# A fused attention and feed-forward kernel: V's conversion placed behind the first norms, the border's loads issued in threes, and the first y tile split ahead

## The chip, the cores and the metric

One core of a Trainium2 chip. The metric is the device time of one execution in microseconds. Before the change, three runs took 1394.03, 1395.40 and 1396.19 us, median 1395.4.

## The reference, cut to what matters

Three layers over 8 batches of 576 tokens, 512 features, all in float32:

```python
kv = einsum('bhsd,bhse->bhde', k, v)              # 8 heads of 64
out = einsum('bhsd,bhde->bhse', q, kv)
x = out / sqrt(mean(out * out, -1) + 1e-6) * g    # norm of each head's row
u = x + (x.T @ U @ V).T                           # U, V of rank 32 over the tokens
z = u + relu(u @ w_ch1) @ w_ch2                   # 512 -> 2048 -> 512
h = gelu(z @ w_in); a, v = split(h)               # 512 -> 1024
result = z + (a * (w_sg @ layernorm(v) + b_sg)) @ w_out
```

## The kernel before, in words

Every matmul that has to keep float32's precision is made of three: an operand is split into a high part (rounded by ScalarE to the type that TensorE reads at full rate) and a low part (the rest, subtracted on VectorE or GpSimd), and `three` (lines 347 to 349) multiplies high by high, high by low and low by high. Some inputs (U, V and the weights) arrive as 64-bit numbers in pairs of 32-bit words; `convert` (line 96) makes float32 of them with two instructions of ScalarE (lines 103, 104), three of VectorE (106 to 108) and an addition on GpSimd (109). `converted` (line 113) runs it, then `flush` empties a queue of one, which holds the split of the weight converted before, and queues its own; so w1 is split (lines 125, 126) only when w2 has been converted. The low half goes to GpSimd for odd weights, to VectorE for even ones.

The program is traced in Python; TensorE's order is the program's own, as written. The other engines and SP, which issues every DMA, get an order from a scheduler that follows the program's and lets a ready instruction pass one that isn't ready, except where `behind` pins an instruction to the one traced before it on its engine (all of `convert` and of the weights' splits is pinned). On the chip each engine runs its list in order, and SP's list is one queue.

**Attention, 0 to about 85 us for the first two batches.** `att_kv(b, ps)` forms a pair of heads' k-v product; `load_kv(b, p)` loads its operands, from the third batch on into two buffers `kvm` that alternate. `put_kv` copies the products to `kvbd`. `att_x(b, c)` (line 264) multiplies one of five chunks of queries with it into a PSUM tile of four buffers; ScalarE squares it (276, into `sq`, one buffer) and copies it out (277), VectorE reduces the square (278). `att_root` (281) is a reciprocal square root in eleven small VectorE instructions. `att_norm` (289) scales a chunk (295) and splits it (300, 301). `att_t` multiplies it with U into `tp`. `att_u(b, d)` (321) transposes a chunk back, adds the product with V (`v4`, line 336) and splits the result u for the next matmul. U is converted and stored by `store_u` at the start, V's two halves right behind it, each converted and then stored by `store_v` (375: a copy on ScalarE, a subtraction on GpSimd), all ahead of the first `att_x`. The batches' work is then mixed by a list of steps written out by hand (`PERIOD`, and `FIRST` for batch 0): X is `att_x` of the next batch, K `att_kv` of the one after it, T `att_t`, D `att_u`, and U is half of a block of the first feed-forward matmul, `ch1` (12 matmuls of 288 columns, with weight block U-number // 2).

**Products, 330 to 545 us.** The other ten blocks of the first feed-forward matmul go through a scheme of seven products for eight (Strassen's) over 25 units; the results y go to DRAM. Meanwhile the weights of the second matmul are converted, stored to DRAM and, from the last pairs on, some are loaded back by `load_w2` (682). Blocks of u come back into a tile `u32` of two buffers.

**The border at 545 us and the second matmul, to about 945 us.** `steps` (773) goes over nine blocks of 512 tokens and eight y tiles each (two features blocks, [128, 2, 512]). `load_y` (743) loads one and splits it: a Relu on ScalarE (752) and one instruction on VectorE (753). `ch2` runs 24 matmuls of 512 columns for a tile. In the first block the tiles start at 4; tiles 4 and 5 lie in `y_at`, loaded during the products into one of the two u32 buffers, and are split at the border. `load_z1` (739) loads a block of u into the other. Behind it stand eight weight loads, and then the y tiles from the third on, in three buffers. The third layer follows; nothing of it is touched.

Of the kernel before, what the change touches and what calls it, by code (L numbers as in the profile page):

```python
# [26 lines left out]
P = 128  # L27
# [32 lines left out]
def tile_kernel(ctx: ExitStack, tc: tile.TileContext, kvm, kvr, qt, gcol, uv, w12,  # L60
# [21 lines left out]
    def in_turn(*chains):  # L82

        end = object()
        while chains:
            chains = [steps for steps in chains if next(steps, end) is not end]
# [32 lines left out]
    def flush():  # L119
        while queue:  # L120
            queue.pop(0)()
# [28 lines left out]
    def slot(i, shape, dt, name):  # L150

        return px["wa" if i < 14 else "xa"].tile([P] + shape, dt, tag=f"s{i}", name=f"{name}{i}")
# [111 lines left out]
    def att_x(b, c):  # L264

        n = rows(c)
        if c == 0:
            at_s["ss", b] = small(b, "ss", 0)
            nc.gpsimd.memset(at_s["ss", b][64:, 4], 1.0)
        ps = pm.tile([P, H, D], F32, tag="ar", bufs=4, name="xps")  # L270
        for p in range(NP):
            mm(ps[:n, 2 * p:2 * p + 2, :], q_t[b, p][:, c * P:c * P + n], kvbd[:, p, :],  # L272
               start=True, stop=True)
        xn = xn_of(b, c)
        sq = ap.tile([P, H, D], F32, tag="sq", name="sq")
        nc.scalar.activation(sq[:n], ps[:n], AF.Square)
        nc.scalar.activation(xn[:n], ps[:n], AF.Copy)
        nc.vector.tensor_reduce(at_s["ss", b][:n, c], sq[:n], AX.X, ALU.add)
        at_s["x", b, c] = xn

    def att_root(b):
        ss = at_s.pop(("ss", b))
        y, t = (small(b, n, i) for i, n in ((1, "ny"), (2, "nt")))
        a, y2, t2 = (i.rearrange("p w h -> p (w h)") for i in (ss, y, t))
        nc.vector.tensor_scalar(a, a, 1.0 / D, EPS, ALU.mult, ALU.add)
        in_turn(rsqrt(y2, t2, a))
        at_s["y", b] = y
# [87 lines left out]
    def store_v(c, x):  # L375
        nc.scalar.activation(v4[:, c], x, AF.Copy)
        nc.gpsimd.tensor_sub(v4[64:96, c], x[64:96], v4[64:96, c].bitcast(F32))
# [104 lines left out]
    tmp_u = next_tmp()[:, :nu]  # L482
    in_turn(convert(uvr[0][:, :nu], tmp_u))
    store_u(tmp_u)
    tmp_v = [slot(i, [2, DM], F32, "tmpv")[:, 0, :HS] for i in (6, 7)]
    for h, (r, t) in enumerate(zip((uvr[0][:, nu:], uvr[1]), tmp_v)):
        in_turn(convert(r, t))
        store_v(slice(h * HS, (h + 1) * HS), t)
    att_kv(0, list(range(NP)))
    put_kv(0)  # L490
    for p in range(NP):
# [6 lines left out]
    for f in range(1, NA):  # L498
        load_w(f, 0)
    att_root(0)  # L500
    att_kv(1, list(range(NP)))
    put_kv(1)
    att_norm(0, (0, 1))
    for cs in ((0, 1), (2, 3), (4,)):
        if cs[0]:
            att_norm(0, cs)
        for c in cs:
            att_t(0, c)
        for c in cs:
            att_x(1, c)  # L510
        if cs[0] < 4:
            split_w(cs[0] // 2)
    for p in range(2):
        load_kv(2, p)
    for d in range(ND):
        att_u(0, d)
    att_root(1)
    for p in range(NP):
        load_q(2, p)
    split_w(2)  # L520
    att_norm(1, (0, 1))
    split_w(3)

    PERIOD = "X0 X1 X2 X3 U X4 U U K0 U K1 U T0 T1 U U T2 T3 U U T4 U K2 U K3 U D0 D1 D2 D3".split()
    FIRST = "U U U K0 U K1 U T0 T1 U U T2 T3 U U T4 U K2 U K3 U D0 D1 D2 D3".split()
    for b in range(B):
        n, n2 = (i if i < B else None for i in (b + 1, b + 2))
        i = 0
# [161 lines left out]
    while units:  # L690
        n = 3 if len(units) == 3 else 2
        two, units = units[:n], units[n:]
        a, b = two[0], two[-1]
        if n == 3:
            for s in "a5 a1 b5 b1 a3 a6 b3 b6 c5 c1 a7 b7 a2 c3 c6 b2 a4 c7 b4 c2 c4".split():
                two["abc".index(s[0])].product(int(s[1]))
                if s == "b7":
                    for f in range(12, 16):
                        load_w2(f)
        else:  # L700
            for x, p in ((a, 5), (a, 1), (b, 5), (b, 1), (a, 3), (a, 6), (b, 3), (b, 6), (a, 7), (b, 7),
                         (a, 2), (b, 2), (a, 4), (b, 4)):
                x.product(p)
        if b.j == len(BLOCKS) - 1 and b.i in (0, 1):
            y = up.tile([P, ND, S], F32, tag="u32", bufs=2, name="y0")
            y_at.append(y.rearrange("p d s -> p (d s)")[:, :2 * 2 * BT].rearrange("p (a f t) -> p a f t", a=2, f=2))
            for k in range(2):
                nc.sync.dma_start(y_at[0][:, k], yd[0][:, 8 + 2 * k:10 + 2 * k])
        if b.j == len(BLOCKS) - 1 and b.i == 1:
            for f in range(8, 12):  # L710
                load_w2(f)
    flush()
    pha.close()
# [27 lines left out]
        nc.sync.dma_start(zt[b], ud[b])  # L741

    def load_y(j, i):
        if j == 0 and i in (4, 5):
            y = y_at[0][:, i - 4]
        else:
            y = y_next.pop() if y_next else bp.tile([P, 2, BT], F32, tag="y", bufs=3, name="yr")
            nc.sync.dma_start(y, yd[j][:, 2 * i:2 * i + 2])
        k = i % 2
        yx = yx_at.pop(k) if k in yx_at else bp.tile([P, 2, 2, BT], F32R, tag=f"yx{k}", name="yx")  # L750
        yh, yl = yx[:, 0], yx[:, 1]
        nc.scalar.activation(yh, y, AF.Relu)  # L752
        nc.vector.scalar_tensor_tensor(yl, y, 0.0, yh.bitcast(F32), ALU.max, ALU.subtract)  # L753
        for k in range(2):
            ys[j, 2 * i + k] = yh[:, k], yl[:, k]
# [15 lines left out]
                nc.sync.dma_start(zd[b], zt[b])  # L771

    steps = [(j, (i + 4) % 8) for j in range(NB) for i in range(8)]
    load_y(*steps[0])
    px["wb"] = wb = ph1.enter_context(tc.tile_pool(name="wb", bufs=1, side="left", reuse_waits="tile"))
    load_z1(0)
    load_y(*steps[1])
    for f in range(8):
        load_w2(f)
    for at_, (j, i) in enumerate(steps):  # L780
        if 2 <= at_ + 1 < len(steps):
            load_y(*steps[at_ + 1])
        step = at_ % 8
        if step == 0 and j + 1 < B:
            load_z1(j + 1)
        for k in range(2):
            ch2(j, 2 * i + k, step == 0 and k == 0, step == 7 and k == 1)
        if j == 0 and step == 5:
            raws = prepare_sg()
        if j == 1 and step < 5:  # L790
            split_sg(step, raws[step])
        if j == NB - 2 and step in (0, 1, 2, 3, 4, 5):
            if step == 0:
                load_wio(0)
            load_wio(step + 1)
            split_wio(step)
        if j == NB - 1:
            if 1 <= step < 7:
                if step < 6:
                    load_wio(step + 6)  # L800
                split_wio(step + 5)
            elif step == 7:
                flush()
            if step >= 3 and step < 7:
                split_z(0, step - 3, zt[order[0]][:, step - 3], nc.vector)
        if step == 7:
            z_out(j)
# [277 lines left out]
```

## Time and profile before

| | |
|---|---|
| median of 3 runs | 1395.4 us |
| the profiled execution's own time | 1394.67 us |
| its span in the trace | 1392.7 us |
| mean granted clock of TensorE | 0.992 |
| busy: TensorE, VectorE, ScalarE, GpSimd | 97%, 55%, 39%, 20% of the span |
| DMA | 199.44 MB, 143 GB/s on average |

The profile is one execution. An engine that isn't busy either waits for another (the trace names the instruction that released it, by the tile that it writes and its line) or has nothing in its list. A matmul is pipelined: its duration overlaps the next one's start, so the distance from start to start is the rate. PEld is TensorE's weight load. "clock" is the share of the 2.4 GHz that TensorE was granted; 0.5 is its lower level, 1.2 GHz.

### The profile page before, as it was taken

The numbers are of one execution on the slowest core, as the hardware profiler recorded it, in microseconds if no ns is written. First come the engines' busy times: TensorE is split into PE (matmuls) and PEld (weight loads), VectorE is DVE, ScalarE is ACT, GpSimd is POOL, SyncE is SP. The second block draws the span as 40 slices with busy tenths as digits, with TensorE's granted clock in tenths as the row PEclk, the third lists the DMA queues.
The fourth block names the chain that finished last, engine by engine and source line by source line (L and its number), as shares of the span: only waits on it lengthen the run. The fifth ranks groups of instructions, "written<-read, shape, count | busy, mean of one in ns | idle before, by whom it ended". The sixth has DMA issues, their size and how long they took to land.

```text
span 1392.7 us, 20749 instructions
## 1 busy us (share of the span) xinstructions
PE 1346.4 (97%) x8050; PEld 1177.5 (85%) x8050; DVE 771.3 (55%) x1405; ACT 536.5 (39%) x888; POOL 284.2 (20%) x268
## 2 busy tenths in 40 slices
PE   5799999999999999899999999999999999999998
PEld 4689999997777788688888888888999999999998
DVE  3757777755766732222322223456676775775874
ACT  3656656654554532212112122454333333423321
POOL 1211111100111100200000000336253453543332
PEclk9899999999999999999999999999999999999999
DMA  9556665355766777635434554631020120110001
GB/s 325 189 165 215 220 215 179 132 174 194 252 228 223 243 268 276 238 96 170 146 118 159 163 169 145 210 122 44 1 68 19 51 69 18 52 44 26 35 17 52
DMA packets 86930, 199.44 MB, mean 143 GB/s; under 512 B 12208, under 2 KB 33456, under 8 KB 85040
## 3 DMA queue, kind: packets, MB, share of 16 engines
q1 hardware_dynamic: 86832, 198.12, 42.9%
q8 instruction: 63, 1.03, 0.3%
q14 instruction: 35, 0.29, 0.1%
HBM read 126.00 MB, written 72.09 MB: 142 GB/s over the span
## 4 chain that ended last, share of the span: by engine, by line
PE 83%; DVE 5%; DMA 3%; ACT 2%; issue 1%; POOL 1%; SPq 0%; DVEq 0%; ACTq 0%; POOLq 0%
PE acc L348 9%; PE acc L347 9%; PE acc L349 9%; PE uso L936 8%; PE uso L957 6%; PE uso L848 5%; PE c L347 3%; PE c L348 3%; PE c L349 3%; PE y L347 3%; PE y L348 3%; PE y L349 3%; PE v L347 2%; PE v L348 2%; PE v L349 2%; PE xps L272 2%
## 5 line engine op out<-in xcount | busy, mean ns | idle before, releaser
L347 PE MATMUL acc<-yx,w 128*128 128x512 f32 x576 | 225.3, 391 | 5.9 <-ACT yx L752 5.9
L348 PE MATMUL acc<-yx,w 128*128 128x512 f32 x576 | 225.7, 392 | 1.5 <-DVE yx L753 1.5
L753 DVE SCALAR_TENSOR_TENSOR yx<-yr,yx 128x1024 fp32r<-128x1024 f32 x70 | 86.1, 1230 | 254.2 <-ACT yx L752 249.8
L349 PE MATMUL acc<-yx,w 128*128 128x512 f32 x576 | 225.3, 391 | 0.0
L752 ACT ACTIVATE yx<-yr 128x1024 fp32r<-128x1024 f32 x70 | 74.3, 1061 | 286.9 <-PE acc L349 267.0
L347 PEld LDWEIGHTS acc<-yx,w 128*128 128x128 f32 x576 | 108.8, 189 | 29.3 <-ACT yx L752 6.6
L348 PEld LDWEIGHTS acc<-yx,w 128*128 128x128 f32 x576 | 108.8, 189 | 24.7 <-DVE yx L753 2.1
L349 PEld LDWEIGHTS acc<-yx,w 128*128 128x128 f32 x576 | 108.9, 189 | 22.7
L349 PE MATMUL c<-uh,w 128*128 128x288 f32 x384 | 114.0, 297 | 6.6 <-POOL w L126 6.6
L347 PE MATMUL c<-uh,w 128*128 128x288 f32 x384 | 117.2, 305 | 0.0
L348 PE MATMUL c<-ul,w 128*128 128x288 f32 x384 | 114.1, 297 | 1.8 <-DVE ul L344 1.8
L848 PE MATMUL uso<-zh,wio 128*128 128x288 f32 x512 | 94.1, 298 | 0.8 <-DVE g2u L856 0.7
L957 PE MATMUL uso<-gh,wio 128*128 128x288 f32 x512 | 93.1, 296 | 0.0
L109 POOL TENSOR_TENSOR tmp<-tmp,wior 128x512 int32<-128x512 int32 x12 | 15.7, 1307 | 332.2 <-DVE tmp L108 287.2
L957 PEld LDWEIGHTS uso<-gh,wio 128*128 128x128 f32 x512 | 77.9, 188 | 2.3 <-issue 0.2
L347 PE MATMUL y<-T,c 128*128 128x512 f32 (+1 forms) x200 | 75.3, 377 | 4.0 <-DVE y L595 3.7
L848 PEld LDWEIGHTS uso<-zh,wio 128*128 128x128 f32 x512 | 76.3, 188 | 3.4 <-PE uso L936 1.4
L349 PEld LDWEIGHTS c<-uh,w 128*128 128x128 f32 x384 | 72.6, 189 | 7.1 <-POOL w L126 7.1
L348 PEld LDWEIGHTS c<-ul,w 128*128 128x128 f32 x384 | 72.6, 189 | 3.9 <-DVE ul L344 3.0
L347 PEld LDWEIGHTS c<-uh,w 128*128 128x128 f32 x384 | 72.5, 189 | 3.2 <-issue 1.0
L349 PE MATMUL y<-T,c 128*128 128x512 f32 (+1 forms) x200 | 74.5, 372 | 0.0
L348 PE MATMUL y<-T,c 128*128 128x512 f32 (+1 forms) x200 | 74.4, 372 | 0.0
(206 smaller groups left out, 2912.4 us busy)
## 6 DMA issues: line engine op xcount, KB each, us to landing
yr<-yd SPq DMA_DIRECT2D x70, 512.0 KB, 3.6
yd<-y SPq DMA_DIRECT2D x92, 256.0 KB, 3.5
kvm<-kvm_dram SPq DMA_DIRECT2D x28, 512.0 KB, 4.6
raw<-w_dram SPq DMA_DIRECT2D x26, 512.0 KB, 4.2
q<-qt_dram SPq DMA_DIRECT2D x32, 288.0 KB, 4.6
ud<-ut SPq DMA_DIRECT2D x32, 288.0 KB, 2.2
z<-ud SPq DMA_DIRECT2D x8, 1152.0 KB, 6.9
out_dram<-ot SPq DMA_DIRECT2D x31, 288.0 KB, 2.1
```

The lines of the kernel that those rows point to most:

```text
L109: yield behind(nc.gpsimd.tensor_add(t, t, low))
L272: mm(ps[:n, 2 * p:2 * p + 2, :], q_t[b, p][:, c * P:c * P + n], kvbd[:, p, :], start=True, stop=True)
L347: mm(ps, ah, bh, start=start, stop=False, **kw)
L348: mm(ps, ah, bl, start=False, stop=False, **kw)
L349: mm(ps, al, bh, start=False, stop=stop, **kw)
L752: nc.scalar.activation(yh, y, AF.Relu)
L753: nc.vector.scalar_tensor_tensor(yl, y, 0.0, yh.bitcast(F32), ALU.max, ALU.subtract)
L848: mm(ps[:, e, :HS], a[:, s], c[:, halves[e]], start=(d == 0 and i == 0), stop=(d == ND - 1 and i == 2))
L936: mm(ps[:, e, :HS], a[:, s], w[:, halves[e]], start=(c == 0 and i == 0), stop=(c == NC - 1 and i == 1))
L957: mm(ops[d][:, e, :HS], a[:, s], c[:, f, halves[e]], start=(f == 0 and i == 0), stop=(f == ND - 1 and i == 2))
```

## The change

Six edits. The sums of squares of the first batch get a second `sq` buffer, in a stretch of the tile `spare[4]` that is free then. V's conversion moves from the start to behind the first two chunks' norms, with both halves interleaved, and its two stores move behind `split_w(1)`; a `flush` is added there, so that w1 is split at once. `split_w(2)` and `split_w(3)` move ahead of `att_root(1)`. In `FIRST`, K2 and K3 move ahead of the T steps. At the border: tile 4 of the first block is split during the last three units' products, into a tile that takes the second u32 buffer; the block of u is loaded later; of the weight loads, those of 11 and 14, 15 move back by a stage, and the loads at the border (14, 15, the block of u, 0 to 7) are issued two first and then three with each step, with the y tile of the next step ahead of the three. The second block of u is loaded at step 3 in place of step 0.

```diff
--- before.py
+++ after.py
@@ -272,7 +272,10 @@
             mm(ps[:n, 2 * p:2 * p + 2, :], q_t[b, p][:, c * P:c * P + n], kvbd[:, p, :],
                start=True, stop=True)
         xn = xn_of(b, c)
-        sq = ap.tile([P, H, D], F32, tag="sq", name="sq")
+        if b or c % 2 == 0:
+            sq = ap.tile([P, H, D], F32, tag="sq", name="sq")
+        else:
+            sq = spare[4][:, 2700:2700 + DM].rearrange("p (h d) -> p h d", h=H)
         nc.scalar.activation(sq[:n], ps[:n], AF.Square)
         nc.scalar.activation(xn[:n], ps[:n], AF.Copy)
         nc.vector.tensor_reduce(at_s["ss", b][:n, c], sq[:n], AX.X, ALU.add)
@@ -482,10 +485,6 @@
     tmp_u = next_tmp()[:, :nu]
     in_turn(convert(uvr[0][:, :nu], tmp_u))
     store_u(tmp_u)
-    tmp_v = [slot(i, [2, DM], F32, "tmpv")[:, 0, :HS] for i in (6, 7)]
-    for h, (r, t) in enumerate(zip((uvr[0][:, nu:], uvr[1]), tmp_v)):
-        in_turn(convert(r, t))
-        store_v(slice(h * HS, (h + 1) * HS), t)
     att_kv(0, list(range(NP)))
     put_kv(0)
     for p in range(NP):
@@ -498,9 +497,12 @@
     for f in range(1, NA):
         load_w(f, 0)
     att_root(0)
+    tmp_v = [slot(i, [2, DM], F32, "tmpv")[:, 0, :HS] for i in (6, 7)]
+    uv_in = [convert(r, t) for r, t in zip((uvr[0][:, nu:], uvr[1]), tmp_v)]
     att_kv(1, list(range(NP)))
     put_kv(1)
     att_norm(0, (0, 1))
+    in_turn(*uv_in)
     for cs in ((0, 1), (2, 3), (4,)):
         if cs[0]:
             att_norm(0, cs)
@@ -510,19 +512,23 @@
             att_x(1, c)
         if cs[0] < 4:
             split_w(cs[0] // 2)
+        if cs[0] == 2:
+            for h, t in enumerate(tmp_v):
+                store_v(slice(h * HS, (h + 1) * HS), t)
+            flush()
     for p in range(2):
         load_kv(2, p)
     for d in range(ND):
         att_u(0, d)
+    split_w(2)
+    split_w(3)
     att_root(1)
     for p in range(NP):
         load_q(2, p)
-    split_w(2)
     att_norm(1, (0, 1))
-    split_w(3)
 
     PERIOD = "X0 X1 X2 X3 U X4 U U K0 U K1 U T0 T1 U U T2 T3 U U T4 U K2 U K3 U D0 D1 D2 D3".split()
-    FIRST = "U U U K0 U K1 U T0 T1 U U T2 T3 U U T4 U K2 U K3 U D0 D1 D2 D3".split()
+    FIRST = "U U U K0 U K1 U K2 U K3 T0 T1 U U T2 T3 U U T4 U U D0 D1 D2 D3".split()
     for b in range(B):
         n, n2 = (i if i < B else None for i in (b + 1, b + 2))
         i = 0
@@ -694,8 +700,14 @@
         if n == 3:
             for s in "a5 a1 b5 b1 a3 a6 b3 b6 c5 c1 a7 b7 a2 c3 c6 b2 a4 c7 b4 c2 c4".split():
                 two["abc".index(s[0])].product(int(s[1]))
+                if s == "c1":
+                    yx = up.tile([P, ND, S], F32R, tag="u32", bufs=2, name="yx0")
+                    yx = yx.rearrange("p d s -> p (d s)")[:, :4 * BT].rearrange("p (a k t) -> p a k t", a=2, k=2)
+                    nc.scalar.activation(yx[:, 0], y_at[0][:, 0], AF.Relu)
+                    nc.vector.scalar_tensor_tensor(yx[:, 1], y_at[0][:, 0], 0.0, yx[:, 0].bitcast(F32),
+                                                   ALU.max, ALU.subtract)
                 if s == "b7":
-                    for f in range(12, 16):
+                    for f in range(11, 14):
                         load_w2(f)
         else:
             for x, p in ((a, 5), (a, 1), (b, 5), (b, 1), (a, 3), (a, 6), (b, 3), (b, 6), (a, 7), (b, 7),
@@ -707,7 +719,7 @@
             for k in range(2):
                 nc.sync.dma_start(y_at[0][:, k], yd[0][:, 8 + 2 * k:10 + 2 * k])
         if b.j == len(BLOCKS) - 1 and b.i == 1:
-            for f in range(8, 12):
+            for f in range(8, 11):
                 load_w2(f)
     flush()
     pha.close()
@@ -741,8 +753,8 @@
         nc.sync.dma_start(zt[b], ud[b])
 
     def load_y(j, i):
-        if j == 0 and i in (4, 5):
-            y = y_at[0][:, i - 4]
+        if j == 0 and i == 5:
+            y = y_at[0][:, 1]
         else:
             y = y_next.pop() if y_next else bp.tile([P, 2, BT], F32, tag="y", bufs=3, name="yr")
             nc.sync.dma_start(y, yd[j][:, 2 * i:2 * i + 2])
@@ -771,17 +783,21 @@
                 nc.sync.dma_start(zd[b], zt[b])
 
     steps = [(j, (i + 4) % 8) for j in range(NB) for i in range(8)]
-    load_y(*steps[0])
+    for k in range(2):
+        ys[0, 8 + k] = yx[:, 0, k], yx[:, 1, k]
     px["wb"] = wb = ph1.enter_context(tc.tile_pool(name="wb", bufs=1, side="left", reuse_waits="tile"))
-    load_z1(0)
     load_y(*steps[1])
-    for f in range(8):
-        load_w2(f)
+    later_loads = [lambda f=f: load_w2(f) for f in (14, 15)] + [lambda: load_z1(0)] + [lambda f=f: load_w2(f) for f in range(8)]
+    later_loads.pop(0)()
+    later_loads.pop(0)()
     for at_, (j, i) in enumerate(steps):
         if 2 <= at_ + 1 < len(steps):
             load_y(*steps[at_ + 1])
+        for _ in range(3):
+            if later_loads:
+                later_loads.pop(0)()
         step = at_ % 8
-        if step == 0 and j + 1 < B:
+        if step == (0 if j else 3) and j + 1 < B:
             load_z1(j + 1)
         for k in range(2):
             ch2(j, 2 * i + k, step == 0 and k == 0, step == 7 and k == 1)
```

## Rows read from the trace of the kernel before

**Rows 1.** Waits of TensorE: who, for whom; total us, times, longest us.

```profile
PE c L349 <- POOL w L126: 6.6, 2, 6.2
PE acc L347 <- ACT yx L752: 5.9, 2, 4.5
...
PE acc L348 <- DVE yx L753: 1.5, 2, 0.8
```

**Rows 2.** Timeline of ScalarE, 0 to 82 us: start, duration, instruction, [idle before].

```profile
16.50 0.44 ACT L103 ACTIVATE tmpv<-uv 128x288 f32<-128x288 f32 x1
...
22.48 0.44 ACT L376 ACTIVATE v<-tmpv 128x288 fp32r<-128x288 f32 x1 [1.27 <-POOL tmpv L109]
...
27.04 0.59 ACT L276 ACTIVATE sq<-xps 64x512 f32<-64x512 f32 x1 [0.32 <-DVE spare L278]
```

**Rows 3.** Timeline of VectorE, 0 to 82 us.

```profile
17.67 0.46 DVE L108 SCALAR_TENSOR_TENSOR tmpv<-uv,tmpv 128x288 int32<-128x288 int32 x1
...
27.66 0.68 DVE L278 TENSOR_REDUCE spare<-sq 64x8 f32<-64x512 f32 x1 [0.72 <-ACT sq L276]
...
31.70 1.89 DVE L295 TENSOR_TENSOR spare<-spare 128x512 f32<-128x512 f32 x3
```

**Rows 4.** Timeline of TensorE, 0 to 82 us.

```profile
14.53 7.86 PE L272 MATMUL xps<-kvbd,q 128*128 128x128 f32 x40 [1.22 <-DMA q<-qt_dram]
...
33.11 0.79 PE L310 MATMUL tp<-xh,u 128*128 128x512 f32 x1 [5.58 <-ACT xh L300]
...
61.38 0.61 PE L349 MATMUL c<-uh,w 128*128 128x288 f32 x1 [6.22 <-POOL w L126]
```

**Rows 5.** Timeline of GpSimd, 0 to 82 us.

```profile
18.27 0.80 POOL L109 TENSOR_TENSOR tmpv<-tmpv,uv 128x288 int32<-128x288 int32 x1 [2.40 <-DVE tmpv L108]
...
57.40 2.71 POOL L109 TENSOR_TENSOR tmp<-tmp,spare 128x512 int32<-128x512 int32 x1 [2.72 <-DMA raw<-w_dram]
60.07 1.25 POOL L126 TENSOR_TENSOR w<-tmp,w 128x512 fp32r<-128x512 f32 x1
```

**Rows 6.** Stretches: length, busy PE, PEld, DVE, ACT, POOL; clock, DMA share, GB/s.

```profile
30.00:37.00 7.00, 3.54 (x11) 2.75 (x12) 6.76 (x16) 2.50 (x4) 0.00 (x0) 0.52 1.01 381
37.00:50.00 13.00, 10.99 (x71) 8.62 (x71) 10.70 (x20) 11.24 (x22) 2.91 (x2) 1.00 0.27 90
61.00:64.50 3.50, 3.12 (x20) 2.84 (x22) 2.44 (x5) 2.08 (x4) 0.33 (x1) 0.52 0.10 40
...
549.00:552.50 3.50, 3.50 (x10) 2.67 (x10) 0.33 (x1) 0.00 (x0) 0.00 (x0) 0.51 1.02 412
552.50:561.00 8.50, 8.30 (x37) 6.55 (x35) 0.00 (x0) 0.00 (x0) 0.00 (x0) 1.00 1.02 419
...
566.00:570.00 4.00, 3.42 (x9) 2.75 (x10) 1.75 (x2) 1.25 (x2) 1.41 (x1) 0.57 0.53 159
```

**Rows 7.** Timeline of TensorE at the border, 543.5 to 574 us.

```profile
546.99 0.50 PE L347 MATMUL acc<-yx,w 128*128 128x512 f32 x1 [1.42 <-ACT yx L752]
...
565.32 0.50 PE L347 MATMUL acc<-yx,w 128*128 128x512 f32 x1 [4.52 <-ACT yx L752]
```

**Rows 8.** Timeline of SP's queue at the border, 536 to 600 us.

```profile
546.70 3.35 SPq L685 DMA_DIRECT2D w<-wd  x7
```

**Rows 9.** Tile kvm, 0 to 60 us; then line L172, 60 to 95 us.

```profile
DMA to landing us min/median/max: 3.4/6.4/10.6
...
DMA to landing us min/median/max: 3.7/4.0/5.2
```

**Rows 10.** Timeline of TensorE, 0 to 82 us, around the first K1.

```profile
65.08 0.40 PE L347 MATMUL c<-uh,w 128*128 128x288 f32 x1
...
66.87 0.69 PE L255 MATMUL kvps<-kvm 128*64 128x64 f32 x16
```

**Rows 11.** The page's costliest groups: the split of a y tile.

```profile
L753 DVE SCALAR_TENSOR_TENSOR yx<-yr,yx 128x1024 fp32r<-128x1024 f32 x70 | 86.1, 1230 | 254.2 <-ACT yx L752 249.8
...
L752 ACT ACTIVATE yx<-yr 128x1024 fp32r<-128x1024 f32 x70 | 74.3, 1061 | 286.9 <-PE acc L349 267.0
```

## Prediction

> **What bounds the kernel now.** I read the list of TensorE's waits first. TensorE is nearly always busy (the table above), so a change that leaves the matmuls alone can only win back waits, or time at the low clock. The list says where they are: c on a w of GpSimd, one wait of 6.2 us, and two groups on yx [rows 1], where the last product hands over to the second feed-forward matmul; near the top of it also tp on an xh of ScalarE [rows 4]. What else the list has is the first key loads, four waits on a y of VectorE in the products, which the change does not touch, and smaller ones. So there are two places, the first 80 us and the border at 545 us. I followed each wait backwards.
>
> The wait of tp, 5.58 us before 33.11 [rows 4]: the query products are all issued by 14.53 + 7.86 = 22.39, but the last sum of squares ends at 27.66 + 0.68 = 28.34, and the norm starts at 31.70 [rows 3]. ScalarE is what lies between [rows 2]: from 16.50 to 22.48 + 0.44 it works on V's two halves or waits for them (1.27 us before the last copy), with products ready and one chunk copied out between; the later chunks wait about 0.3 us each for the one sq buffer, as the row at 27.04 shows.
>
> The wait of c, 6.22 us before 61.38 [rows 4]: the low half of w1 comes from GpSimd's L126 at 60.07, and that is queued behind L109 of w2, which starts at 57.40 [rows 5]. w1 is not stored until w2 has been converted.
>
> The clock [rows 6]: with each of these waits comes a stretch at about half the clock (0.52 in 30 to 37 and in 61 to 64.5), the 1.2 GHz level, while in 37 to 50 it is 1.00.
>
> The border: TensorE waits 1.42 us before its first acc matmul at 546.99, for a split that begins only when the products are over, and 4.52 us before 565.32 for the third y tile [rows 7]. Its load stands in SP's queue behind seven w loads from 546.70 [rows 8] and the block of u, and in 549 to 552.5 all DMA engines are busy at 412 GB/s [rows 6]. The list has 5.9 us in two waits on ScalarE's yx and 1.5 in two on VectorE's [rows 1], 7.4 in all. Two stretches at half clock follow (0.51 and 0.57).
>
> **The change, part by part.**
>
> *V's conversion goes behind the first norms; sq has two buffers.* ScalarE is then free when the first chunk is ready. TensorE's last chunk ends at 22.39; one square (0.59), one reduction (0.68) and handovers of 0.1 to 0.2 each put the last sum at 24.0 instead of 28.34. The pace before it (a square and a copy are about 1.1 us a chunk, a chunk of TensorE 7.86/5 = 1.6) doesn't hold it up. Gain 4.4. At 33.1 to 37 TensorE ran at half clock with 3.54 us busy in 7 [rows 6], so up to 1.8 more if it stays at full clock; I take 0.8, because VectorE paces this stretch too.
>
> What moves in: VectorE's six instructions, three for each half, at no more than the 0.46 of the longest kind, L108 [rows 3]: 2.8 us. VectorE is busy 6.76 of 7 us there, 10.70 of 13 in the next stretch [rows 6]. So the cost lies between 0 (the 2.3 us of slack takes it) and 2.8; I take 1.1, since the slack stands behind the full stretch, not in it. ScalarE's four conversions and two copies (0.44 each [rows 2]) find it busy 2.50 of 7 [rows 6]: nothing, and if that cover goes, at most 2.7 us. GpSimd's four, two adds and two subtractions of 0.80 [rows 5], now run beside dense VectorE work: between 0 and 4 x 0.80 = 3.2 us; the add at 57.40 took 2.71 where L126, of the same size, took 1.25 [rows 5], so something does meet there. I take 0.3, nearer to nothing, since V is first needed when att_u begins, after five T's and five X's.
>
> The Trainium skill, SBUF — State Buffer, section "Who interferes with whom", says that a VectorE instruction with two SBUF inputs and a GpSimd instruction that reads SBUF take a shared port as a lock: one blocks for the other's whole length. The 2.71 us add agrees; by that rule VectorE would lose up to 3.2 us and the sum would be 2.9 higher, a rival below.
>
> Part sum: -4.4 - 0.8 + 1.1 + 0.3 = **-3.8** (-6.2 to +1.6).
>
> *w1 is stored right after its conversion; w2 and w3 are converted ahead of root(1).* The flush puts L126 of w1 ahead of L109 of w2. w1's own add is over before w2's begins, so its low half no longer waits for anything of w2, and the 6.22 us go. The half clock in 61 to 64.5 goes with them: TensorE is busy 3.12 us there [rows 6], half of it, 1.5. V's two subtractions come ahead of w1's on GpSimd, 1.6 us, a quarter of the wait that goes (bound: 1.6 left of it). What is late next is w2 and w3, now converted earlier; root(1) and its norms move back by two conversions, covered because T0 comes after K3. **-7.7**.
>
> *K2 and K3 move forward in the first batch.* Here a wait is added. Key block 2 is loaded into the buffer that K0 frees. From K0's end to K2 there are now U, K1, U: 1.8 + 0.9 + 1.8 = 4.5 us (a U from 65.08 to 66.87; a K is the 0.69 shown and four matmuls more, an estimate) [rows 10]. Such a load lands in 3.7 to 5.2 us later on, but in up to 10.6 us when the queues are full [rows 9], and the four raw loads of w6 to w9 are about at that time. TensorE takes its work in the order written, so U5, K3 and the T's stand behind a late K2. Bounds 0 and 10.6 - 4.5 = 6.1; I take **+2**, nearer to the later loads, since K3's wait runs inside K2's.
>
> *The border.* The first y tile is split during the products: ScalarE 1.06 and VectorE 1.23 us [rows 11], between evictions that leave both engines idle for more than half of the stretch; taken at 0 (bound 1.2, one split late). So the first two waits go, and with the loads in threes the y tiles stand ahead of most w loads. Gain at most 7.4 of waits plus what the clock took, 3.5 x 0.49 and 4 x 0.43, 3.4: 10.8. What remains is DMA. A w or y tile is 0.52 MB, a block of u 1.18. Ahead of the third y tile stand w14, w15, u, w0, w1: with itself 3.8 MB, 9.2 us at 412 GB/s, so it lands near 555 if the loads begin at 545.7; its split takes 1.1 and TensorE asks at 545.6 + 2 x 5.5 = 556.6. (A step is 24 matmuls of 8.5/37 = 0.23 [rows 6]; 545.6 is 546.99 - 1.42.) The next y tile needs 2.1 MB more, landing at 560, with the ask at 562.1 less 1.1. That is just in time. But u's load now waits until the y block is free (its second split, about 545.9 + 1.06 + 1.23 = 548.2), and what is behind it on SP waits as well: 0 to 5 us, of which I take 2. **-8.8** (-10.8 to -5).
>
> **Sum.** -3.8 - 7.7 + 2 - 8.8 = -18.3. The profiled execution took 1394.7 us (span 1392.7 and 2.0 around it), so 1376.4; the median of the runs is 0.7 above that execution, so I predict **1377**.
>
> **Rivals.**
> (1) *GpSimd holds VectorE up.* GpSimd's V work costs VectorE the full 3.2 and the slack is no cover: with V's 2.8 in full beside it the first part becomes -4.4 - 0.8 + 2.8 + 3.2 = +0.8, total -13.7, 1382. For it: the 2.71 us add. Against it: V's tiles are half as long as w's. 8%.
> (2) *SP is blocked at the border.* u's load stands third, everything behind it waits until 548.2, and the y tiles come late two or three times; the half clock returns. The border gives back 5 more: -13.3, 1382. For it: DMA has no room (412 GB/s already). Against: the third y tile has three w loads less in front of it. 13%.
> (3) *The waits only change their names*: att_u waits for V's low half where tp waited for xh, w1's subtraction is ordered late on GpSimd all the same, and y tiles arrive at the old pace. The change would then not do what it says; within 2.8 us of 1395. 6%.
> (4) *Slower: K2 and K3 starve.* Their loads are queued behind the raw loads of w6 to w9 and the stores; TensorE stands at K2 with everything behind it, then at K3, and runs at half clock after that. One wait at the worst landing is 6.1; both in full with 3.4 of half clock are 15.6. It decides only if the two waits exceed 18.3 + 2 + 2.8 = 23 us together, 16 us of landing for each load against the worst of 10.6 seen; at 25 us the time would be 1400. 7%.
> The forecast itself, both ends gained: 66%.
>
> **Numbers.** About 0.2%, 2.8 us, is what a measurement of this kernel can tell from no change. Faster: 66 + 8 + 13 = 87%; the same 6%; slower 7%. The range goes from both ends at their best (-6.2 - 7.7 + 0 - 10.8, and 1 us more for small waits on w and xh that the new order may cover: -25.7, 1369) to K2 at its worst with rival 1 and the border at its poorest (+0.8 - 7.7 + 6.1 - 5 = -5.8: 1390). It holds the forecast and rivals 1 and 2.
>
> **What would show it.** Right: tp's first matmul near 28 us, no c wait on GpSimd's w, granted clock 1.00 from 37 us to the border, the first acc matmul within 0.3 us of the last y matmul, a third y tile landed by 556. Wrong: a kvps wait on a kvm load over 3 us, an ups wait on V, VectorE's adds near 1.3 us beside V's GpSimd work, or an acc wait of 4 us behind the load of u.

## The result and the profile after

Four runs took 1379.02 to 1382.52 us, median **1380.97**; the kernel before has 1395.8 in the same comparison. The ratio is 0.9895 (95% interval 0.9878 to 0.9912), 14.8 us less. The profiled execution took 1381.16 (span 1379.1). The forecast of 1377 is 4 us too low, and faster was right.

Three marks show where the time went (starts in the trace, before, then after). The third x product of batch 2, which both kernels reach with the same work done, starts at 93.39 and 86.43: the start gives 7.0. The first acc matmul comes at 546.99 [rows 7] and 538.81, 8.2 earlier, of which 1.4 is its own wait: 6.8 come through the products. The first matmul of the third layer comes at 951.50 and 938.23, 13.3 earlier: the border gives 6.5, that wait included. The profiled executions differ by 13.5 (1394.67 to 1381.16). The marks that the rows above don't show, TensorE's timeline before, then after:

```profile
93.39 2.05 PE L272 MATMUL xps<-kvbd,q 128*128 128x128 f32 x16 [0.28 <-ACT xn L277]
951.50 0.43 PE L848 MATMUL uso<-zh,wio 128*128 128x288 f32 x2
```

```profile
938.23 0.43 PE L864 MATMUL uso<-zh,wio 128*128 128x288 f32 x2
```

The list of TensorE's waits, whole kernel after (who, for whom; total us, times, longest us). The change shifts the line numbers: what is L310 before is L313 here, and L752 is L764.

```profile
PE tp L313 <- ACT xh L303: 4.1, 2, 2.1
...
PE acc L351 <- DVE yx L765: 1.9, 3, 0.8
PE acc L350 <- ACT yx L764: 1.7, 1, 1.7
```

The two groups that led to the border are 3.6 us where they were 7.4 [rows 1], and the c wait on GpSimd's w of 6.22 [rows 4] is gone from the list. The xh wait is smaller but comes twice. TensorE's timeline after, 25 to 102 us, shows the second:

```profile
26.73 0.49 PE L313 MATMUL tp<-xh,u 128*128 128x512 f32 x1 [2.07 <-ACT xh L303]
...
34.71 0.50 PE L313 MATMUL tp<-xh,u 128*128 128x512 f32 x1 [2.07 <-ACT xh L303]
...
48.11 0.40 PE L350 MATMUL c<-uh,w 128*128 128x288 f32 x1 [0.35 <-ACT uh L346]
49.50 0.61 PE L351 MATMUL c<-ul,w 128*128 128x288 f32 x1 [0.99 <-DVE ul L347]
...
66.55 0.69 PE L255 MATMUL kvps<-kvm 128*64 128x64 f32 x16 [1.02 <-DMA kvm<-kvm_dram]
...
86.43 2.05 PE L272 MATMUL xps<-kvbd,q 128*128 128x128 f32 x16 [0.16 <-ACT ut L343]
```

The first norm is 6.4 us early (33.11 before [rows 4]), but the first c matmul only 1.5. TensorE's timeline before has it at

```profile
49.61 0.29 PE L347 MATMUL c<-uh,w 128*128 128x288 f32 x1
```

What ate it is in ScalarE's, GpSimd's and VectorE's timelines after:

```profile
32.95 0.44 ACT L379 ACTIVATE v<-tmpv 128x288 fp32r<-128x288 f32 x1 [4.24 <-POOL tmpv L109]
...
34.05 1.14 ACT L303 ACTIVATE xh<-spare 128x512 fp32r<-128x512 f32 x2
```

```profile
30.22 2.69 POOL L109 TENSOR_TENSOR tmpv<-tmpv,uv 128x288 int32<-128x288 int32 x1 [14.96 <-DVE tmpv L108]
```

```profile
30.36 1.89 DVE L298 TENSOR_TENSOR spare<-spare 128x512 f32<-128x512 f32 x3
```

The scaled chunks for the third and fourth xh are there from 32.3 at the latest (30.36 + 1.89), yet the xh start at 34.05: V's copies are ahead of them in ScalarE's list, and the first waits 4.24 us for GpSimd's sum of V, which took 2.69 us where the same add took 0.80 before [rows 5].

The granted clock, stretches after (length; busy PE, PEld, DVE, ACT, POOL; clock, DMA share, GB/s):

```profile
28.60:32.00 3.40, 3.40 (x15) 3.02 (x14) 3.40 (x10) 0.11 (x1) 1.78 (x1) 0.50 1.03 417
49.00:56.00 7.00, 6.50 (x25) 6.00 (x26) 6.95 (x16) 4.37 (x9) 1.36 (x1) 0.51 0.72 236
```

The half clock at 61 to 64.5 [rows 6] has not gone: a stretch of it now begins at 49, with TensorE busy 6.50 us, so that it costs up to half of that, 3.2. At the border it is gone: 1.00 from 55.9 us to the end. The border after, TensorE's timeline and then SP's queue:

```profile
538.81 0.39 PE L350 MATMUL acc<-yx,w 128*128 128x512 f32 x1
...
550.48 0.50 PE L351 MATMUL acc<-yx,w 128*128 128x512 f32 x1 [0.34 <-DVE yx L765]
557.68 0.50 PE L350 MATMUL acc<-yx,w 128*128 128x512 f32 x1 [1.69 <-ACT yx L764]
558.94 0.50 PE L351 MATMUL acc<-yx,w 128*128 128x512 f32 x1 [0.76 <-DVE yx L765]
565.58 0.51 PE L351 MATMUL acc<-yx,w 128*128 128x512 f32 x1 [0.76 <-DVE yx L765]
```

```profile
541.10 0.43 SPq L760 DMA_DIRECT2D yr<-yd  x1
544.51 0.32 SPq L753 DMA_DIRECT2D z<-ud  x1
...
545.88 0.38 SPq L760 DMA_DIRECT2D yr<-yd  x1
```

The second product starts without a wait, and the four waits of 7.4 us together [rows 1] have become four of 3.55. SP waits 2.9 us for TensorE before it issues the block of u at 544.51 (line 753), with the second loaded y tile, issued at 545.88 and landed at 556.47, behind it.

### The profile page after: what moved, and what is told of

It reads as the page before. It is cut to its first block, busy times and chain, and to the rows that moved or that the text cites. A ratio compares the mean times of both kernels' runs of the same rounds, so it can differ in the third digit from the quotient of the medians.

```text
span 1379.1 us, 20736 instructions
## 1 busy us (share of the span) xinstructions
PE 1345.7 (98%) x8050; PEld 1177.0 (85%) x8050; DVE 771.8 (56%) x1405; ACT 535.4 (39%) x888; POOL 285.6 (21%) x268
## 5 line engine op out<-in xcount | busy, mean ns | idle before, releaser
L764 ACT ACTIVATE yx<-yr 128x1024 fp32r<-128x1024 f32 x70 | 74.3, 1061 | 283.5 <-PE acc L352 256.5
```

## The experiments

Times are of one profiled execution unless several runs are named. Kernels with the same code at a place differ there by up to 2.75 us (third x product of batch 2: 86.43 after, 89.18 in experiment 10, which changes only the border), so of single executions the traces' waits are read, and differences of 3 us. "The x products" in the expectations are that mark.

**1, 2. Each end alone.** In 1 the hunks of the diff from `if s == "c1"` on are undone, in 2 all those ahead of it. Some lines of the edit of 2:

```diff
-            sq = spare[4][:, 2700:2700 + DM].rearrange("p (h d) -> p h d", h=H)
...
-    FIRST = "U U U K0 U K1 U K2 U K3 T0 T1 ...
+    FIRST = "U U U K0 U K1 U T0 T1 ...
```

> The start of the changed kernel with the border of the kernel before. Theory (the two ends are separate, and nothing between them moves): the products end 6.5 us earlier than before, the border keeps its waits of 1.4, 0.8, 4.5 and 0.8 us and both half-clock stretches, and the run is 6 to 8 us faster than before, about 1388.5. Rival (the ends share DMA: what the start frees shows only at the border): less than 4 us in all, or a border wait that differs by more than 1 us from that of the kernel before.

Measured: 1389.32 (four runs), ratio 0.9952 (0.9937 to 0.9967). The trace misses the theory in its parts: the first acc matmul comes at 542.98, 4.0 us earlier and not 6.5; the waits at the border are 1.42, 0.76, 5.84 and 0.47 us; and the clock is at its lower level once, 0.50 from 561 to 566. The 5.84 is 1.3 more than the kernel before has there, which the rival named as a sign of its own.

> The border of the changed kernel with the start of the kernel before. Theory (separate ends): the first acc matmul follows the last product without a wait, the waits left are those on y tiles, 1.7, 0.8, 0.8 and 0.3 us, no half clock, 6 to 8 us faster than before, about 1389. Rival (the ends share DMA): the y waits grow to 4 us again and less than 4 us is won.

Measured: 1386.99 (four runs), ratio 0.9931 (0.9914 to 0.9947). The first acc matmul follows without a wait, the y waits are 0.55, 0.76 and 0.43 us, and no half clock is left there, as in the theory. Against 1396.48 in that comparison the ends are worth 7.2 and 9.5; the whole, 14.8, is about their sum within what the runs can tell. From the first acc matmul to the third layer it is 404.7 us in kernel 1 and 404.5 before, for all the change in single waits. So nothing shows that one end's gain depends on the other, and the start has given less than forecast.

**3. V's conversion back at the start**, the rest as after.

```diff
+    for h, (r, t) in enumerate(zip((uvr[0][:, nu:], uvr[1]), tmp_v)):
+        in_turn(convert(r, t))
+        store_v(slice(h * HS, (h + 1) * HS), t)
     att_kv(0, list(range(NP)))
...
-    in_turn(*uv_in)
```

> The changed kernel with V's conversion and stores back at the start; the second sq buffer, the early store of w1, the order of w2 and w3 and the K steps stay. Theory (the move of V pays at the first norm and is given back because V's two copies stand ahead of the third xh on ScalarE and wait 4.2 us there): tp's first matmul comes 3 to 4 us later than in the changed kernel (30 to 31 us instead of 26.7), but the third tp waits for no xh, and U0's first c matmul comes within 1.5 us of the changed kernel's 48.1. Rival (moving V is worth what it gives at the first norm, 6.4 us): U0's first matmul comes 4 us or more later, at 52 or later.

Measured: 1380.04. TensorE's timeline of this kernel:

```profile
30.77 0.79 PE L313 MATMUL tp<-xh,u 128*128 128x512 f32 x1 [4.25 <-ACT xh L303]
...
47.97 0.40 PE L350 MATMUL c<-uh,w 128*128 128x288 f32 x1 [0.35 <-ACT uh L346]
```

The first norm is 4.0 us later, the first c matmul no later than after (48.11). V's move pays at the norm and gives it all back within 20 us.

**4. V's stores behind the third and fourth xh**, the copies pinned there, the rest as after.

```diff
         if cs[0]:
             att_norm(0, cs)
+        if cs[0] == 2:
+            for h, t in enumerate(tmp_v):
+                store_v(slice(h * HS, (h + 1) * HS), t)
```

> The changed kernel with one thing moved: V's two stores (a copy on ScalarE, a subtraction on GpSimd each) stand behind the norm of chunks 2 and 3, with the copies pinned there, so that ScalarE scales and rounds the third xh before it waits for GpSimd's sum of V. Theory (what holds the start up after the first norm is ScalarE standing in its own list, 4.24 us before V's copy at 32.95, with the third xh behind it): the third tp has its xh 2 to 4 us earlier, TensorE's wait of 2.07 us before 34.71 falls under 1, and the first c matmul comes at 44 to 46.5 instead of 48.11; V's copies then wait for nothing. Rival (VectorE's adds and norms, or GpSimd's 2.69 us addition beside them, pace the start): the wait at 34.71 goes to another tile, and the first c stays within 1 us of 48.11. Whole time by the theory 1377 to 1380, by the rival within 1 us of 1381.

Measured: 1380.77; first c matmul 48.09. ScalarE's, then TensorE's timeline of this kernel:

```profile
31.66 1.23 ACT L303 ACTIVATE xh<-spare 128x512 fp32r<-128x512 f32 x2 [2.42 <-DVE spare L298]
```

```profile
33.41 0.47 PE L313 MATMUL tp<-xh,u 128*128 128x512 f32 x1
...
37.63 0.50 PE L313 MATMUL tp<-xh,u 128*128 128x512 f32 x1 [1.27 <-DVE xh L304]
41.29 0.36 PE L339 MATMUL ups<-v,t 128*128 128x256 f32 x1 [1.77 <-DVE t L319]
```

TensorE's clock from there on, in this kernel and after the change:

```profile
43.50:57.20 13.70, 12.71 (x46) 10.42 (x47) 12.18 (x28) 8.72 (x18) 4.82 (x4) 0.50 0.56 190
```

```profile
43.50:57.20 13.70, 11.76 (x53) 9.69 (x54) 12.14 (x26) 9.27 (x19) 5.02 (x4) 0.75 0.62 212
```

The hold-up was as named: the xh start 2.4 us earlier, and the third tp (33.41) waits for nothing. But the fifth chunk's xh now stands behind V's copies, two new waits come, and from the middle of att_u on the clock is half. At the mark of 48 us nothing is left. The theory is right about the cause and wrong about the price; the rival's numbers hold. What paces the stretch behind it is not shown: TensorE is busy 12.71 of 13.70 us there at 0.50, but VectorE is busy 12.18.

**5. Without the added flush.** And **6, with the conversions of w2 and w3 back** behind root(1) and the first norm, the flush kept.

```diff
             for h, t in enumerate(tmp_v):
                 store_v(slice(h * HS, (h + 1) * HS), t)
-            flush()
```

> The changed kernel without the added flush: w1 is split only when w2 has been converted, as before the change; everything else, V's stores too, stays. Theory (the flush alone takes the 6.2 us wait away, and its price is that the uh of att_u stand behind w1's rounding, which waits 1.48 us for GpSimd): a c wait of 4 to 7 us on GpSimd's w comes back at the third block U, and a stretch at about half clock behind it; the uh no longer wait, so the first c comes 0.5 to 2 us earlier than 48.11; the first acc matmul is 4 to 7 us later than 538.81, the whole time 1385 to 1388. Rival (the earlier conversions of w2 and w3, ahead of root(1), do it by themselves, since w2's conversion now lets w1 go sooner): a c wait under 2 us, the time within 1.5 us of 1381.

Measured: 1380.20. GpSimd's, then TensorE's timeline of kernel 5:

```profile
53.44 1.29 POOL L109 TENSOR_TENSOR tmp<-tmp,spare 128x512 int32<-128x512 int32 x1 [5.44 <-ACT y L367]
54.68 1.28 POOL L126 TENSOR_TENSOR w<-tmp,w 128x512 fp32r<-128x512 f32 x1
```

```profile
56.02 0.40 PE L352 MATMUL c<-uh,w 128*128 128x288 f32 x1 [0.67 <-POOL w L126]
```

The theory falls: the wait is 0.67 us, and the first c matmul, at 48.77, is not earlier either. w1's split is still behind w2's add, but w2 is converted 4 us earlier (53.44 against 57.40 [rows 5]), and that is nearly enough.

```diff
-    split_w(2)
-    split_w(3)
     att_root(1)
...
+    split_w(2)
     att_norm(1, (0, 1))
+    split_w(3)
```

> The changed kernel with the conversions of w2 and w3 back at their places behind root(1) and the first norm, the added flush kept: the counterpart of the run without the flush. Theory (the 6.2 us had one cause, w1's split behind w2's conversion, and either edit alone takes it away; the earlier conversions serve w2 and w3 besides): no c wait on GpSimd's w at the third block U, but one of 1.5 to 4 us on w2 or w3 at a later U, batch 2's x products 1 to 4 us later than 86.43, whole time 1381 to 1385. Rival (the earlier conversions do nothing once the flush is there): no c wait on w over 0.5 us, whole time within 1 us of 1381.

Measured: 1380.50, one wait of c on a w, VectorE's low half of w2:

```profile
62.72 0.40 PE L352 MATMUL c<-uh,w 128*128 128x288 f32 x1 [0.81 <-DVE w L126]
```

Either edit alone takes the 6.2 us away; the second adds under 1 us of waits. Of two edits that I had credited with one sum, either would have done.

**7. K2 and K3 back behind T4**, the rest as after.

```diff
-    FIRST = "U U U K0 U K1 U K2 U K3 T0 T1 U U T2 T3 U U T4 U U D0 D1 D2 D3".split()
+    FIRST = "U U U K0 U K1 U T0 T1 U U T2 T3 U U T4 U K2 U K3 U D0 D1 D2 D3".split()
```

> The changed kernel with the old order of the first batch's steps (T0 to T4 ahead of K2 and K3). Theory A (K2 and K3 stand where the T's would wait for their norms): the wait of 1.0 us on the key load goes, but T0 waits for root(1) and its norms, which now stand behind w2's and w3's conversions; the start of batch 2's queries comes 1 to 4 us later than in the changed kernel. Theory B (the move of K2 and K3 costs its load wait and gives nothing): 1 us earlier than in the changed kernel.

Measured: 1383.87, the third x product 3.2 us later (89.65). GpSimd's, then TensorE's timeline:

```profile
65.38 2.11 POOL L109 TENSOR_TENSOR tmp<-tmp,spare 128x512 int32<-128x512 int32 x1 [5.85 <-DVE tmp L108]
67.45 1.26 POOL L126 TENSOR_TENSOR w<-tmp,w 128x512 fp32r<-128x512 f32 x1
```

```profile
68.76 0.40 PE L352 MATMUL c<-uh,w 128*128 128x288 f32 x1 [2.72 <-POOL w L126]
```

Without K2 and K3 in front, TensorE reaches w3 before its low half is there: w3's split is behind w4's add, the pattern of w1 one pair later. Behind that wait the granted clock is 0.52 from 70.0 to 73.4. So the K's are cover and not cost. The size was expected, the waiter was not.

**8. w1's store behind att_u(0)**, the rest as after.

```diff
                 store_v(slice(h * HS, (h + 1) * HS), t)
-            flush()
...
         att_u(0, d)
+    flush()
     split_w(2)
```

> The changed kernel with the flush that stores w1 moved behind att_u(0), still ahead of the conversion of w2. Theory: w1's rounding no longer stands ahead of uh in ScalarE's list, so the four uh come 1 to 2 us earlier and the first c at 46 to 47.2 instead of 48.11, while w1's low half is still there when the third U asks for it (no c wait on GpSimd's w over 0.5); whole time 1379 to 1380.5. Rival (the uh are paced by TensorE's transposes and VectorE's ups, not by ScalarE's list): the first c within 0.4 us of 48.11, and w1, now later, makes a c wait of 1 to 3 us; whole time 1381 to 1384.

Measured: 1382.15, and the first c matmul at 48.17, both as the rival has them, but without its c wait on w1. The granted clock is 1.00 from 39.7 to 67.0 in this kernel, the half clock at 49 is gone, and yet nothing is won. TensorE's timeline, SP's waits from 50 to 70 us, and SP's queue say why:

```profile
66.74 0.97 PE L255 MATMUL kvps<-kvm 128*64 128x64 f32 x16 [3.40 <-DMA kvm<-kvm_dram]
```

```profile
SPq L370 <- ACT y L367: 7.5, 2, 5.3
```

```profile
61.56 0.81 SPq L370 DMA_DIRECT2D yd<-y  x2
62.87 0.33 SPq L172 DMA_DIRECT2D kvm<-kvm_dram  x1
```

K1 is over by 58.4, but the load into its buffer goes out at 62.87: it stands behind a y store, which waits for ScalarE's copy of y, which stands behind two xh of the second batch's norm. K3 starts between 65.8 and 68.2 in every kernel with the new start and this order of steps. It waits for its load 2.69 us in kernel 1 and 1.56 in kernel 3, so what was won before it is lost again there; in kernels 4 and 5 the wait is 0.47 and 0.25, and in kernel 6 there is none, since the c wait on w2 has put the K's later. That this load alone kept the time of experiments 3 to 6 where it was is likely, not shown.

**9. K0 K1 and K2 K3 in pairs.**

```diff
-    FIRST = "U U U K0 U K1 U K2 U K3 T0 T1 ...
+    FIRST = "U U U K0 K1 U U U K2 K3 T0 T1 ...
```

> The changed kernel with the first batch's list of steps at U U U K0 K1 U U U K2 K3 T0 T1 in place of U U U K0 U K1 U K2 U K3 T0 T1: the loads for K2 and K3 stand in SP's queue ahead of the y stores of the fourth block U. Theory (in every run with the new start K3 begins between 65.8 and 68.2 us whatever came before it, because its load is issued at 62 to 63 us, behind y stores that wait for ScalarE's y copy, which stands behind two xh of the second batch's norm): both loads are issued by 60 us, no kvps wait on a kvm load over 0.3 us; then w3's low half, on GpSimd only at 67.66 us, is the next thing late, a c wait of 1 to 3 us. Whole time 1379.5 to 1381.5. Rival (the loads themselves are slow because all DMA engines are busy): K2 or K3 waits 1 us or more although its load is issued before 60.

Measured: 1380.82. SP's queue, then TensorE's timeline:

```profile
57.43 0.33 SPq L172 DMA_DIRECT2D kvm<-kvm_dram  x1
...
58.46 1.86 SPq L172 DMA_DIRECT2D kvm<-kvm_dram  x1
```

```profile
68.13 0.40 PE L352 MATMUL c<-uh,w 128*128 128x288 f32 x1 [1.47 <-POOL w L126]
73.23 0.50 PE L315 MATMUL tp<-xl,u 128*128 128x512 f32 x1 [1.68 <-DVE xl L304]
```

As the theory has it: no wait on kvm, and w3's low half next, 1.47 us. With it and the 1.68 on xl the third x product is at 88.83, no earlier than after the change.

**10. The block of u loaded at step 3**, the second at step 5, the rest as after.

```diff
-    later_loads = [... for f in (14, 15)] + [lambda: load_z1(0)] + [... for f in range(8)]
+    later_loads = [... for f in (14, 15)] + [... for f in range(8)]
...
+        if at_ == 3:
+            load_z1(0)
```

> The changed kernel with the load of the block of u issued at step 3 instead of third in SP's queue at the border (and the second block's at step 5). Theory (SP stands 2.9 us at the block of u, which goes into the buffer of the first y tile's split and so waits for the matmuls that read it; every y tile behind it comes that much later): SP issues all loads of the first steps without a wait, the second loaded y tile lands 3 us or more earlier than 556.47, the waits of 1.69 and 0.76 us before 557.68 and 558.94 go; whole time 1378 to 1379.5. Rival (DMA is full there, 346 to 416 GB/s from 541.5 to 563, so that the 2.9 us cost nothing and only the order of the tiles counts): the waits move to the y tile behind the block of u with 1.5 to 3 us in sum; whole time within 1 us of 1381.

Measured: 1378.44. The first 30 us of the second product in this kernel, then the same stretch after the change:

```profile
541.10:571.10 30.00, 30.00 (x135) 24.72 (x133) 7.35 (x6) 8.09 (x10) 0.81 (x1) 1.00 1.00 389
```

```profile
538.80:568.80 30.00, 26.46 (x113) 20.47 (x112) 5.33 (x5) 5.57 (x6) 0.00 (x0) 1.00 0.99 377
```

No wait is left (30.00 busy of 30.00). From the first acc to the third layer it is 394.6 us, against 399.4 after (397.6 in kernel 2, with the same code there) and 404.5 before. The second loaded y tile lands 13.6 us after the first acc in place of 17.7. SP's stand explains the smaller part: the DMA engines are full in both (share 0.99 and 1.00), and the 12 GB/s between them are 0.36 MB, 0.9 us. The larger part is the order of the bytes, 1.18 MB of u that are no longer ahead of that tile, 2.8 us at 416 GB/s (an estimate). The two were not tried apart.

**11, 12. All of it.** Kernel 11 has edits 4, 8, 9 and 10, and w3 stored right after its conversion. In kernel 12 the conversions of w4 and w5 come two feed-forward blocks later besides.

```diff
     split_w(3)
+    flush()
     att_root(1)
...
-                if b == 0 and i in (1, 3, 5):
-                    if i < 5:
-                        split_w(4 + i // 2)
-                    else:
-                        flush()
+                if b == 0 and i in (5, 7):
+                    split_w(i // 2 + 2)
+                    if i == 7:
+                        flush()
```

> The changed kernel with the u block's load at step 3, V's stores behind the third and fourth xh, w1's store behind att_u(0), K0 K1 and K2 K3 in pairs, and w3 stored right after its conversion. Theory (each hold-up is an instruction that stands in an in-order list behind one that waits for another engine, and each of these edits takes one out): no kvps wait on kvm and no c wait on w over 0.5 us, the second batch's last x products at 81.5 to 84.5 instead of 86.43, no wait in the first 60 us of the border; whole time 1373 to 1376. Rival (VectorE's roots and norms pace the start, so the time before the second batch's T steps is fixed): a tp wait of 2 us or more on the second batch's xh, x products within 1 us of 86.43, whole time 1377.5 to 1379, that of the late u load alone.

Measured: 1377.71, with no wait on a w, none on kvm behind the first key loads, and one new one. ScalarE's, then TensorE's timeline of kernel 11:

```profile
68.46 0.63 ACT L125 ACTIVATE w<-tmp 128x512 fp32r<-128x512 f32 x1 [2.12 <-POOL tmp L109]
69.00 1.13 ACT L303 ACTIVATE xh<-xn 128x512 fp32r<-128x512 f32 x2
```

```profile
69.66 0.80 PE L313 MATMUL tp<-xh,u 128*128 128x512 f32 x1 [2.85 <-ACT xh L303]
```

Again an xh behind a weight that waits for GpSimd; the third x product is only at 87.38. The theory's time is missed and all three numbers of the rival hold (a tp wait over 2 us, 87.38, 1377.71); that its reason does not, since ScalarE's list and not VectorE holds the xh, is what kernel 12 tests.

> The kernel with the five edits of the run before (late u load, V's stores behind the xh, w1's store behind att_u(0), K's in pairs, w3 stored at once), and w4 and w5 converted two feed-forward blocks later, so that ScalarE's roundings of them no longer stand ahead of the xh of the second batch's third and fourth chunk. Theory (those xh came at 69.00 because ScalarE waited 3.21 and 2.12 us for GpSimd's sums of w4 and w5 just before, with the scaled chunks there since 63.5): the tp wait of 2.85 at 69.66 and the half clock from 69.5 to 76.4 go, no c wait on w over 1 us takes their place; batch 2's x products end 3 to 5 us earlier than in the run before; whole time 1372.5 to 1375.5, ratio to the kernel before 0.983 to 0.9855. Rival (VectorE paces that stretch and w4 comes late instead): a c wait of 2 us or more on w4 or w5, whole time 1377 to 1380.

Measured: **1373.16** (five runs, 1372.43 to 1374.41), ratio 0.9842 (0.9828 to 0.9855), 22.7 us below the kernel before in its comparison, and the interval lies wholly below that of the change. The third x product is at 83.03, 3.4 before that of the change, and the longest wait from K0 to it is

```profile
70.07 0.40 PE L352 MATMUL c<-uh,w 128*128 128x288 f32 x1 [1.18 <-DVE w L126]
```

so that w4 is now a little late in its turn. The theory holds but for that wait, which is over its 1 us. This kernel has all the edits together; how its gain divides among them was not tried.

## Why the prediction was right, and where it was off

*V's conversion: -3.8 forecast, nothing measured.* The gain at the first norm is there: 4.4 forecast for V's move and the second sq buffer, 6.4 measured (33.11 to 26.73), of which V's move is 4.0 (experiment 3). What failed is "ScalarE's four conversions and two copies ... nothing, and if that cover goes, at most 2.7 us". I counted how long ScalarE is busy and not what stands behind a copy that waits: the wait was 4.24 us, longer than the bound. The price of GpSimd's work (0.3 taken, to 3.2) was 1.89 on one add of its own, and 0.46 on VectorE (below).

*w1 and the conversions: -7.7.* The 6.22 us wait went, as forecast, and the clock's 1.5 did not: the half clock came earlier in its place, so "granted clock 1.00 from 37 us to the border" is wrong. That "the flush" does it is half the truth: by experiments 5 and 6 either edit would have taken the wait away.

*K2 and K3: +2 forecast, about -3 measured* (one execution: without the move 2.72 us of wait and 3.4 us at half clock behind it, with it 1.02 of wait). This sign was wrong. A late load was seen, 1.02 us, near the bottom of its bounds. That w2 and w3 are "late next" was seen too, but not that the K's in front of them cover w3, though w1 had shown the pattern. The wait itself came from SP's place behind a y store (experiment 8), not from full queues.

*The three together*: -9.5 forecast, -7.0 in the trace, -6.7 by the ratio of experiment 1 (-4.7 at the same mark in its one trace). That they came this near is in part luck: the 3.8 that V's move did not give is made up by the 5 between +2 and -3.

*The border: -8.8 forecast.* Alone it gives -9.6 by its ratio, in the profiled execution of the whole change -6.5. First acc behind the last product, no half clock: right. The 2 us for u's load stood on "until the y block is free (its second split, about ... 548.2)". SP's row shows another release, TensorE's last matmul on the split tile, since the second u32 buffer holds that tile and the load goes into it. The order of the loads was also read one step off: "Ahead of the third y tile stand w14, w15, u, w0, w1" is true of the fourth; the third's load goes out at 541.10, ahead of u, w0 and w1, and its split costs TensorE only 0.34. The wait was 2.9 us and the four y waits together 3.55, so the 2 us was too small by about 1.5, and "just in time" for the fourth tile missed by 1.69. (The poorest case given, -5, does not come out of its terms: -10.8 with the 5 us is -5.8, and with the late split's 1.2 it is -4.6.)

Rival 2 (SP blocked) happened in part: SP stood 2.9 us, the fourth y tile was 1.69 late and others under 0.8, and the half clock that it counted with did not return. Rival 1's mechanism is there, at a small part of its price: VectorE's three instructions took 1.89 us beside GpSimd's add, as before [rows 3], and the add waited for them; but beside GpSimd's subtraction of V, two from 33.75 to 35.29, VectorE lost 0.46 of the 3.2. Its timeline after:

```profile
34.69 1.74 DVE L304 TENSOR_TENSOR xl<-spare,xh 128x512 fp32r<-128x512 f32 x2 [2.44 <-ACT xh L303]
```

Such a pair takes 1.28 before. Rival 3 (the waits only change their names) is what V's move came to by 48 us. Rival 4's starving K's were 1.02 us.

## What to carry to other kernels

On an engine or queue that runs its list in order, price a moved instruction by the wait in front of it and by what is queued behind it, not by its busy time; look for the first instruction behind it that TensorE needs. A wait taken away at one place is worth what the next fixed point downstream lets through: look for that point (in several kernels here a key load at 66 us) before adding gains up, and expect to take out several before the time moves. A copy of the same pattern (a split one conversion late) is likely at the next weight too.

## What had not been expected of the hardware

GpSimd's add of 128x288 took 2.69 us where it overlapped three VectorE instructions of two inputs each, 1.89 us in all, and 0.80 alone [rows 5]: 0.80 + 1.89 = 2.69. It was held for as long as they took, and they did not slow down. The Trainium skill, SBUF — State Buffer, section "Who interferes with whom", describes such a lock; the trace agrees, and shows which of the two gave way here. It is not always GpSimd. At 53.80 GpSimd begins an add of 1.36 us, and a VectorE instruction that begins in it and takes 0.20 us elsewhere takes 1.30. GpSimd's, then VectorE's timeline after:

```profile
53.80 1.36 POOL L109 TENSOR_TENSOR tmp<-tmp,spare 128x512 int32<-128x512 int32 x1 [4.98 <-DVE tmp L108]
```

```profile
53.92 1.30 DVE L93 SCALAR_TENSOR_TENSOR nt<-nt,ss 128x40 f32<-128x40 f32 x1
```

In both places the one that was already at work kept going and the other waited.

The granted clock fell to its lower level, 1.2 GHz, at 49.0 after ten microseconds at 1.00 in which TensorE was busy 8.13 of 10:

```profile
39.00:49.00 10.00, 8.13 (x47) 5.49 (x46) 8.29 (x15) 8.37 (x17) 4.17 (x3) 1.00 0.26 90
```

The one wait over 0.4 us near it is the 0.99 before 49.50 (shown above), which runs from 48.51 across the fall. The stretch at half clock moves, or is missing, between kernels that differ little there: none from 39.7 to 67.0 in experiment 8, 51.0 to 54.4 in experiment 5, 44.0 to 47.4 in kernel 12. What sets it is open.
